# One TensorE loop of sixteen turns for two attention blocks: three units a turn, one accumulating output bank, and buffers of one slot per position

## The chip, the cores and the metric

The kernel runs on one core of one Trainium2 chip. The metric is the device time in microseconds (us). A kernel is executed several times beside the kernel before on the same chip. The profile is of one execution; its span is the time from the first to the last instruction, some 1.8 us less than the device time of the same execution.

## The reference, cut to what matters

Two independent attention blocks are computed for one new token each. Block A reads the whole cache of 8192 positions, block B only the last 2048.

```python
B, Sq, D = 4, 1, 512
Hq, Hkv, Sk, Dh = 32, 8, 8192, 128          # four query heads share one k/v head
q = (x @ wq).reshape(B, Sq, Hq, Dh).transpose(0, 2, 1, 3)
k = repeat(k_cache, 4, axis=1)              # block B: k_cache[:, :, Sk - W:, :], W = 2048
v = repeat(v_cache, 4, axis=1)
p = softmax(einsum("bhqd,bhkd->bhqk", q, k) * Dh ** -0.5)
o = einsum("bhqk,bhkd->bhqd", p, v)
out = o.transpose(...).reshape(B, Sq, Hq * Dh) @ wo
# result: concatenate([block A, block B], axis=-1)
```

In bfloat16 the caches of A are 134 MB, what B reads of its own is 34 MB, and the weights are 17 MB. There is little arithmetic per byte: each byte of K and V is used once.

## The kernel before: the parts that matter

Work is cut into units. A unit of A is one batch and one k/v head: 64 tiles of 128 positions, 2 MB of K and 2 MB of V. For each unit TensorE transposes K (`T`), makes scores (`S`), and later applies the probabilities to V (`PV`). The kernel before runs 8 large units of B first (2 MB of K each, too), then 32 units of A. K and V have four slots each.

```python
NKS, NVS, NKT, NPT = 4, 4, 4, 4
K_sb = sb("K_sb", [128, NKS, NT, DH], BF16)       # NT = 64 tiles
V_sb = sb("V_sb", [128, NVS, NT, DH], BF16)
KTB, STB, OTB, OPB = [0, 1, 2], [3, 4], [5, 6], 7 # PSUM banks: K transposed, scores, PV, output
...
TOKENS = [("T", 0), ("T", 1), ("OT",), ("T", 2), ("T", 3), ("S", 0), ("S", 1), ("X",),
          ("T", 4), ("T", 5), ("S", 2), ("S", 3), ("PV", 0), ("PV", 1), ("OL",),
          ("T", 6), ("T", 7), ("S", 4), ("S", 5), ("PV", 2), ("PV", 3), ("S", 6), ("S", 7), ("OPJ",)]
...
def sp_K(u):                                      # a slot is free when the unit four back is transposed
    waits = [("T", tjob_idx[(u - NKS, NB - 1)])] if u >= NKS else []
...
def sp_V(u):                                      # ... or when its PV is done
    waits = [("PV", (u - NVS) * NQ + NQ - 1)] if u >= NVS else []
```

The remaining tokens (`OT`, `OL`, `X`) stand for small jobs on the outputs and on the query projections. Most A units already run in a TensorE loop of four units a turn; the front and the end are unrolled. The output product `OPJ` of a group of four units is 4 matmuls of 512 columns for A, 16 for B.

## Time and profile before

| | before |
|---|---|
| device time, median (range) | 449.75 us (449.16 to 450.03, 4 runs) |
| span of the profiled run | 447.8 us |
| bytes read from memory | 184.56 MB |
| TensorE busy | 373.4 us, 83% of the span |
| mean granted TensorE clock | 0.797 |

The page cuts the span into 40 slices. Each digit is the busy share of a slice in tenths. PEclk is the granted TensorE clock in tenths, DMA the busy share of the 16 DMA engines, GB/s what they moved.

```profile
PE   0685199899676999988998998899889998988997
PEclk9996569989886899866596689867875986788596
DMA  8999999999999999999999999999999999999991
GB/s 337 411 415 438 413 421 415 420 421 423 423 422 421 425 422 425 424 429 427 427 427 430 430 424 426 430 428 427 429 426 427 426 430 429 426 424 430 430 403 65
```

The DMA row is what to look at: it is full from the second slice to the last but one. The TensorE row is nearly as full, yet it is not the limit. The groups of instructions (line, engine, operation, output<-input, shapes, count | busy us, mean ns | idle us just before them and what ended it) show transposes waiting for K:

```profile
L332 PE MATMUL ps<-identf,K_sb 128*128 128x128 f32 x1280 | 217.1, 329 | 32.9 <-DMA K_sb<-in_A_k_cache_dram 17.5
L483 PE MATMUL ps<-W,OL 128*4 128x512 bf16 x60 | 22.5, 537 | 4.8 <-DMA W<-in_B_wo_dram 4.8
```

The chain of work that ended last says the same by its shares of the span:

```profile
DMA 54%; PE 35%; issue 4%; ACT 3%; DVE 2%; POOL 0%; ACTq 0%; POOLq 0%
```

The DMA issues (SPq is the queue of SyncE, which issues the loads; count, KB each, median us from issue to landing) show how deep the queue is. A load waits about 30 us behind others, some 12 MB:

```profile
K_sb<-in_A_k_cache_dram SPq DMA_DIRECT2D x32, 2048.0 KB, 32.0
V_sb<-in_A_v_cache_dram SPq DMA_DIRECT2D x31, 2048.0 KB, 36.0
```

The busy times of the engines in stretches (us from the span's start; TensorE, its weight loads, DVE, ACT, POOL, then granted clock, DMA share, GB/s) give the rate of the stream and its end:

```profile
0.00:14.00 14.00, 0.00 (x0) 0.00 (x0) 0.18 (x4) 1.28 (x1) 2.03 (x12) 1.00 0.87 345
60.00:180.00 120.00, 102.38 (x1973) 88.60 (x1970) 61.43 (x136) 50.95 (x56) 10.34 (x30) 0.88 1.01 422
180.00:420.00 240.00, 217.52 (x3823) 202.49 (x3824) 105.46 (x243) 104.20 (x119) 22.14 (x71) 0.76 1.01 428
440.00:448.00 8.00, 5.17 (x126) 4.10 (x126) 2.08 (x7) 0.42 (x1) 0.46 (x2) 0.50 0.01 3
```

Data stop at 440 us. The last 7.8 us are TensorE's backlog and the output. The timeline (start, length, engine, line, ...; in brackets the idle time just before and what ended it, where `issue` stands for a time in which the engine waited for nothing that the profile shows) shows the backlog, 118 matmuls of the last two units:

```profile
440.17 3.31 PE L397 MATMUL ps<-PT,V_sb 128*128 128x4 bf16 x118 [0.82 <-issue]
443.79 1.86 PE L474 MATMUL ps<-W,OTg 128*4 128x256 bf16 x8 [0.31 <-DVE OTg L592]
```

The clock deserves a look too. A pair of transpose jobs (x8) takes 1.07 us when TensorE has been busy, and 1.97 us after it stood waiting for K:

```profile
285.80 1.07 PE L332 MATMUL ps<-identf,K_sb 128*128 128x128 f32 x8
289.84 1.97 PE L332 MATMUL ps<-identf,K_sb 128*128 128x128 f32 x8 [1.38 <-DMA K_sb<-in_A_k_cache_dram]
```

### The profile page before, as it was taken

The page shows a single profiled execution, that of the slowest core. Times are in us where ns is not written, and L with a number is a line of the kernel's source. Part 1 is how long each engine was busy: PE and PEld are TensorE (multiplying, and loading weights), DVE is VectorE, ACT ScalarE, POOL GpSimd, SP SyncE. Part 2 cuts the span into 40 slices and gives each one's busy share as a digit, 9 for nine tenths or more (in the row PEclk, how much of TensorE's full clock was granted, in tenths as well). Part 3 has the DMA queues.
Part 4 walks back from the last instruction along what each step waited for, and adds up shares of the span by engine and source line. Part 5 has one row for each costly group of instructions (what it writes and reads, how often), then busy time and mean ns, then how long its engine had stood idle before and what let it go on. Part 6 is the DMA issues. An engine that isn't in the chain of part 4 may idle for free.

```text
span 447.8 us, 14767 instructions
## 1 busy us (share of the span) xinstructions
PE 373.4 (83%) x6783; PEld 339.4 (76%) x6783; DVE 195.9 (44%) x451; ACT 179.2 (40%) x202; POOL 40.1 (9%) x126
## 2 busy tenths in 40 slices
PE   0685199899676999988998998899889998988997
PEld 0685199768561898878898887879878987878896
DVE  0354055656440455434363444344443544344363
ACT  1163045435330464434264434334442543435261
POOL 1100000001100011000010001000110100010010
PEclk9996569989886899866596689867875986788596
DMA  8999999999999999999999999999999999999991
GB/s 337 411 415 438 413 421 415 420 421 423 423 422 421 425 422 425 424 429 427 427 427 430 430 424 426 430 428 427 429 426 427 426 430 429 426 424 430 430 403 65
DMA packets 17270, 185.01 MB, mean 413 GB/s; under 512 B 1860, under 2 KB 2392, under 8 KB 4824
## 3 DMA queue, kind: packets, MB, share of 16 engines
q1 hardware_dynamic: 15096, 178.27, 94.4%
q10 hardware_dynamic: 2080, 6.30, 3.5%
q8 instruction: 22, 0.36, 0.3%
q14 instruction: 8, 0.07, 0.0%
q0 software_dynamic: 64, 0.01, 0.0%
HBM read 184.56 MB, written 0.01 MB: 412 GB/s over the span
## 4 chain that ended last, share of the span: by engine, by line
DMA 54%; PE 35%; issue 4%; ACT 3%; DVE 2%; POOL 0%; ACTq 0%; POOLq 0%
DMA K_sb<-in_A_k_cache_dram 41%; PE ps L332 19%; DMA W<-in_A_wq_dram 7%; DMA W<-in_B_wo_dram 6%; PE ps L397 6%; PE ps L371 5%; PE ps L483 3%; ACT KT_sb L341 3%; PE ps L278 1%; DVE KT_sb L340 1%; DVE Dt L543 0%; DVE M L505 0%; ACT PT L554 0%; PE ps L474 0%; PE ps L438 0%
## 5 line engine op out<-in xcount | busy, mean ns | idle before, releaser
L341 ACT ACTIVATE KT_sb<-ps 128x1024 bf16<-128x1024 bf16 x160 | 163.0, 1023 | 244.9 <-PE ps L332 243.1
L332 PE MATMUL ps<-identf,K_sb 128*128 128x128 f32 x1280 | 217.1, 329 | 32.9 <-DMA K_sb<-in_A_k_cache_dram 17.5
L332 PEld LDWEIGHTS ps<-identf,K_sb 128*128 128x128 f32 x1280 | 179.0, 170 | 46.2 <-DMA K_sb<-in_A_k_cache_dram 18.6
L340 DVE COPY KT_sb<-ps 128x512 int32<-128x512 int32 x160 | 110.4, 690 | 138.9 <-PE ps L332 137.7
L397 PE MATMUL ps<-PT,V_sb 128*128 128x4 bf16 (+1 forms) x2560 | 76.2, 165 | 3.6 <-DMA V_sb<-in_A_v_cache_dram 1.8
L371 PEld LDWEIGHTS ps<-RQc,KT_sb 128*128 128x128 bf16 x2048 | 72.9, 100 | 4.5 <-ACT KT_sb L341 1.2
L371 PE MATMUL ps<-RQc,KT_sb 128*128 128x8 bf16 x2048 | 74.3, 167 | 0.9 <-ACT KT_sb L341 0.8
L397 PEld LDWEIGHTS ps<-PT,V_sb 128*128 128x128 bf16 x2560 | 70.8, 97 | 3.9 <-DMA V_sb<-in_A_v_cache_dram 2.0
L575 POOL PARTITION_ALL_REDUCE LB<-L x40 | 17.3, 432 | 155.2 <-DVE L L566 155.2
L514 POOL PARTITION_ALL_REDUCE MB<-M x32 | 11.9, 371 | 173.3 <-DVE M L505 173.3
L483 PE MATMUL ps<-W,OL 128*4 128x512 bf16 x60 | 22.5, 537 | 4.8 <-DMA W<-in_B_wo_dram 4.8
L592 DVE TENSOR_TENSOR OTg<-ps,RL 128x4 bf16<-128x4 f32 (+1 forms) x40 | 6.9, 173 | 40.2 <-PE ps L397 40.2
L505 DVE TENSOR_REDUCE M<-ps 128x4 f32<-128x256 f32 (+1 forms) x40 | 19.1, 477 | 10.8 <-PE ps L371 10.8
L566 DVE TENSOR_REDUCE L<-PT 128x4 f32<-128x256 bf16 (+1 forms) x40 | 21.9, 547 | 3.3 <-ACT PT L554 2.8
L371 PE MATMUL ps<-RQB,KT_sb 128*128 128x16 bf16 x512 | 18.6, 171 | 2.1 <-issue 1.2
L371 PEld LDWEIGHTS ps<-RQB,KT_sb 128*128 128x128 bf16 x512 | 17.9, 99 | 3.0 <-issue 1.5
L554 ACT ACTIVATE PT<-Dt 128x256 bf16<-128x256 f32 (+1 forms) x40 | 18.1, 452 | 4.0 <-DVE Dt L543 2.0
L483 PEld LDWEIGHTS ps<-W,OL 128*4 128x4 bf16 x60 | 5.6, 104 | 15.3 <-issue 8.7
L278 PE MATMUL ps<-xT,W 128*128 128x4 bf16 x256 | 7.4, 165 | 10.9 <-DMA W<-in_A_wq_dram 10.6
L278 PEld LDWEIGHTS ps<-xT,W 128*128 128x128 bf16 x256 | 7.0, 101 | 11.1 <-DMA W<-in_A_wq_dram 10.7
L543 DVE TENSOR_TENSOR Dt<-ps,MB 128x256 f32<-128x256 f32 x32 | 13.3, 415 | 0.5 <-POOL MB L514 0.5
L257 PE MATMUL ps<-ident,xo_sb 4*128 4x4 bf16 x8 | 0.6, 170 | 14.2 <-POOL identf L617 14.2
(49 smaller groups left out, 64.6 us busy)
## 6 DMA issues: line engine op xcount, KB each, us to landing
K_sb<-in_A_k_cache_dram SPq DMA_DIRECT2D x32, 2048.0 KB, 32.0
V_sb<-in_A_v_cache_dram SPq DMA_DIRECT2D x31, 2048.0 KB, 36.0
K_sb<-in_B_k_cache_dram SPq DMA_DIRECT2D x16, 1024.0 KB, 28.2
V_sb<-in_B_v_cache_dram SPq DMA_DIRECT2D x16, 1024.0 KB, 28.2
W<-in_B_wq_dram SPq DMA_DIRECT2D x1, 4096.0 KB, 12.9
W<-in_A_wq_dram SPq DMA_DIRECT2D x1, 4096.0 KB, 30.0
W<-in_A_wo_dram ACTq DMA_DIRECT2D x8, 512.0 KB, 10.5
W<-in_B_wo_dram SPq DMA_DIRECT2D x1, 2048.0 KB, 29.1
```

The costliest lines, as they stand in the source:

```text
L278: ins = pe.matmul(out=bk[:, hl * Bn:(hl + 1) * Bn], lhsT=W1wq[:, c, hq * DH:(hq + 1) * DH], rhs=xT[:, P, c, :], start=(c == 0), stop=(c == ...
L332: ins = pe.transpose(out=bkf[:, pi * 128:(pi + 1) * 128], in_=K_sbf[:, slot, t0:t0 + 2, :].rearrange("p t d -> p (t d)"), identity=identf[ ...
L340: return e.tensor_copy(out=KT_sb.bitcast(I32)[:, tj % NKT, :], in_=bkf.bitcast(I32)[:, :])
L341: return e.activation(out=KT_sb[:, tj % NKT, :], in_=bk[:, :], func=ACTF.Copy)
L371: ins = pe.matmul(out=stb[:, t * CPT:(t + 2) * CPT], lhsT=ktv[:, pi, :, e], rhs=rhs, start=(e == 0), stop=(e == 1))
L397: ins = pe.matmul(out=otb[:, s * CPT:(s + 1) * CPT], lhsT=V_sb[:, vs, t, :], rhs=pt_cols(u, t * CPT, CPT), start=(j == 0), stop=(j == J - 1))
L483: ins = pe.matmul(out=opb[0:Bn, 0:D], lhsT=OL[:, i // REP, i % REP, :], rhs=wo_view[:, wg + i // REP, i % REP, :], start=(P == 1 and first ...
L505: return dve.tensor_reduce(out=M1[:, 0:NC].rearrange("p (s h) -> p s h", h=CPT), in_=stb[:, 0:NT * CPT].rearrange("p (s j h) -> p s h j", ...
L543: return dve.tensor_tensor(out=Dt[:, 0:NT * CPT].rearrange("p (s j h) -> p s j h", s=S, h=CPT), in0=stb[:, 0:NT * CPT].rearrange("p (s j h ...
L554: return act.activation(out=PT[:, u % NPT, 0:NW], in_=Dt[:, 0:NW], func=ACTF.Exp, scale=scale)
L566: return dve.tensor_reduce(out=L1[:, 0:NC].rearrange("p (s h) -> p s h", h=CPT), in_=PT[:, u % NPT, 0:NT * CPT].rearrange("p (s j h) -> p ...
L575: return pool.partition_all_reduce(LB[:, 0:NC], L1[:, 0:NC], channels=128, reduce_op=ReduceOp.add)
```

## The change

The intent is to make the whole TensorE program regular: 16 turns of the same loop, each with two units of A and one of B. A unit of B becomes two batches of one head (32 tiles, 1 MB of K). K and V get one slot per position of the turn: 160 tiles in place of 256. The scores get one bank in place of two, and K transposed gets four banks. Output weights are staged, copied by the Pool engine once a turn, and applied by 16 matmuls of 128 columns into one bank that accumulates over the whole kernel. Both query weights (8.4 MB) are loaded first. The diff, cut to its core (`...` marks cuts):

```diff
-    NKS, NVS, NKT, NPT = 4, 4, 4, 4
+    NPOS = 3
+    NTURN = 2 * HKV
+    NU = NPOS * NTURN
...
+    for t in range(NTURN):
+        g, bh = t // 2, t % 2
+        units.append(dict(P=0, g=g, b=2 * bh, CPT=REP, NT=NT))
+        units.append(dict(P=0, g=g, b=2 * bh + 1, CPT=REP, NT=NT))
+        units.append(dict(P=1, g=g, bh=bh, CPT=2 * REP, NT=NTB))
...
-        K_sb = sb("K_sb", [128, NKS, NT, DH], BF16)
-        V_sb = sb("V_sb", [128, NVS, NT, DH], BF16)
+        NTT = 2 * NT + NTB
+        K_sb = sb("K_sb", [128, NTT, DH], BF16)
+        V_sb = sb("V_sb", [128, NTT, DH], BF16)
...
-        KTB = [0, 1, 2]
-        STB = [3, 4]
-        OTB = [5, 6]
-        OPB = 7
+        KTB = [0, 1, 2, 3]
+        STB, OTB, EVB, OPB = 4, 5, 6, 7
...
+        def pe_OPJ(t):
+            ...
+                for P in range(2):
+                    for r in range(2):
+                        for j in range(4):
+                            ins = pe.matmul(out=banks_f[OPB][32 * j:32 * j + 8, 0:128], lhsT=OL[:, P, r, :],
+                                            rhs=Wfix[:, P, r, 128 * j:128 * j + 128], start=False, stop=False)
...
+        TOK_A = [("T", 0), ("T", 1), ("T", 2), ("T", 3), ("PV", 0), ("S", 0), ("S", 1), ("T", 4), ("T", 5), ("S", 2), ("S", 3),
+                 ("T", 6), ("T", 7), ("S", 4), ("S", 5), ("PV", 1), ("S", 6), ("S", 7)]
+        TOK_B = [("T", 0), ("T", 1), ("OT",), ("T", 2), ("T", 3), ("PV", 0), ("OL",), ("S", 0), ("S", 1), ("PV", 1), ("S", 2), ("S", 3), ("OPJ",)]
...                                            # in unit u the PV is that of unit u - 2
         def sp_K(u):
+            op("sp", dma(...), waits=[("T", tj_of[(u - NPOS, nt // 8 - 1)]) if u >= NPOS else None], inc=("K", u))
         def sp_V(u):
+            w = [pv_last(u - NPOS) if u >= 1 else None]
...
+        for P in range(2):
+            op("sp", dma(WQ_sb[P]..., WQ[P]...), inc=("wq", P))
+        for u in range(NU):
+            if u >= 2 and u < NU - 1:
+                sp_V(u - 2)
+            if u == NU - 2:
+                sp_K(u)
+                sp_K(u + 1)
+                continue
+            if u == NU - 1:
+                sp_V(u - 2)
+                sp_V(u)
+                sp_V(u - 1)
+                continue
+            sp_K(u)
+            if u % 6 == 3:
+                wo_load(u // 6)
```

The loads in the last lines go through one queue, in order, and a load that must wait for a free slot blocks all behind it. Units are numbered from 0 to 47 below; 45 and 46 are the A units of the last turn, 47 is its B unit, 44 the B unit before.

## The prediction

> **What bounds it now.** DMA. The page's slices show the 16 DMA engines at "9" from the second slice to the last but one, 403 to 438 GB/s, for 184.56 MB of input that cannot shrink. In the windows, 0 to 12 us average 345 GB/s, 180 to 420 us 423 to 432, and the stream ends near 440 us. The Trainium skill (DMA: Bandwidth & Descriptors, Specifications) gives a fabric ceiling of 435 GB/s; the trace sits 2% under it. The chain of waits agrees: 41% hops of K_sb from A_k_cache of about 30 us, transfers issued three units ahead. TensorE is 83% busy but not the limit: with a backlog a 64-tile unit takes 7.1 us; waiting for K it falls to half clock (8 transposes 1.97 us instead of 1.07) and takes about 9.6. DMA needs 9.9 us for an A unit (4.19 MB at 427 GB/s).
>
> **What the change does.** Bytes, tiles and shapes of T, S and PV stay. Removed: the unrolled TensorE front, the 60 output matmuls of 512 columns (537 ns, 22.5 us in all), one of two score banks, and buffer depth: K and V go from 256 tiles each to 160 (two A slots, one B). Added: 16 output matmuls of 128 columns and a Pool copy of weights a turn, both Wq (8.4 MB) loaded ahead of the first K, semaphore bookkeeping.
>
> TensorE per turn, estimated: 2 x 9.6 + 5 + 2 = 26 us at low clock, 20 at full. DMA per turn: 11 MB, 25.9 us. So DMA still binds, and TensorE speeds up when it lags.
>
> Does the shallow buffer starve DMA? When K of a first A unit lands, 6.3 MB (14.8 us) are still queued; the next issue comes when that unit's last PV is done, 9 to 10 us later, 2 more to data. It holds, with 3 us margin. Elsewhere 17.3 us are queued. The score bank now waits for the previous subtraction, but max, all-reduce, subtract and evictions (about 2.6 us) fit under 16 transposes and half a PV (2.7 us).
>
> **Off steady state.** Start: 15.7 MB go unblocked, to about 40 us. Unit 0 begins when both projections are done, about 29 us, and frees V1 and K3 at 37 to 39: a hole of 0 to 1.5 us. End: V of the last B unit waits for the previous B's PV, late in the next-to-last unit; 3.1 MB (7.4 us) are queued, a hole of about 2.5 us. Against that, the tail shrinks: before, 118 PV matmuls (3.3 us) ran after the last data and 8 us passed; after, I estimate 5 to 6.
>
> Sum: +0.5 +2.5 -2.5, a wash. Removed TensorE work buys nothing; it hides under DMA.
>
> **Prediction:** 449.5 us, range 445.5 to 456. Faster by over 2%: 0.03; within 2%: 0.90; slower by over 2%: 0.07.
>
> **What would show it.** DMA at 9 in nearly every slice, about 425 GB/s; K issue-to-landing falling from 32 us to about 15; one dip near 38 us and one near 430; TensorE idle before transposes put down to DMA of K; chain still DMA with shorter hops; output matmuls under 20 us.
>
> **What would make it wrong.** Slower: TensorE at half clock plus bookkeeping over 2 us a turn would eat the margin, the queue running dry once a turn (16 x 1 to 2 us, 465 to 480 us); or the Pool copy delays the sums' all-reduce and, through in-order DVE, the evictions. Faster: the early stretch (412 to 423 GB/s) reaching 430 when A and B mix, at most 5 us.

## The result, and the profile after

The time after is 452.35 us (451.73 to 453.84, 4 runs), against 449.75 us before. The ratio is 1.0065, with a 95% interval of 1.0045 to 1.0086. Ratios here are the mean time of one kernel's runs over that of the other's runs of the same rounds, so they are not quite the ratio of the medians quoted. The change is slower by about 3 us, which is well within 2%, and 452.35 lies in the predicted range.

Slices of the page, to be held against those of before:

```profile
PE   0369897896859699796959989697987968696895
PEclk9999789796879757895876959587787968798876
DMA  8999999999999999999999999999999999999945
GB/s 350 417 427 386 416 428 426 429 432 424 422 430 428 415 426 435 428 421 425 430 424 415 407 434 425 430 425 422 422 427 429 428 427 425 424 432 401 425 192 217
```

DMA is full again, except near the end, where two slices moved 192 and 217 GB/s. The fourth slice, 386, is a smaller dent. TensorE, meanwhile, shows digits of 6 and 7 where before it had 8 and 9. The groups say why: the transposes now wait 61.2 us, 59.2 of it for K of A, and the output product costs 7.0 us in place of 22.5 (2 x 0.6 us for the last head group come on top).

```profile
L326 PE MATMUL ps<-identf,K_sb 128*128 128x128 f32 x1280 | 212.4, 327 | 61.2 <-DMA K_sb<-in_A_k_cache_dram 59.2
L491 PE MATMUL ps<-Wfix,OL 128*8 128x128 bf16 x256 | 7.0, 234 | 0.0
```

The chain of waits, in its shares of the span:

```profile
DMA 61%; PE 35%; SPq 1%; DVE 1%; issue 1%; ACT 0%; POOL 0%
```

The DMA issues, in the columns of before:

```profile
K_sb<-in_A_k_cache_dram SPq DMA_DIRECT2D x32, 2048.0 KB, 17.1
V_sb<-in_A_v_cache_dram SPq DMA_DIRECT2D x31, 2048.0 KB, 15.5
```

The chain is more of DMA than before, and the queue is half as deep. The stretches, in the same columns as before:

```profile
0.00:14.00 14.00, 0.00 (x0) 0.00 (x0) 6.60 (x5) 1.28 (x1) 1.71 (x12) 1.00 0.91 368
38.00:44.00 6.00, 5.24 (x110) 5.13 (x107) 3.24 (x7) 3.27 (x5) 0.98 (x3) 1.00 0.95 355
60.00:180.00 120.00, 99.29 (x1953) 95.30 (x1951) 55.96 (x135) 51.81 (x61) 20.91 (x48) 0.80 1.01 427
180.00:420.00 240.00, 198.90 (x3892) 190.25 (x3889) 110.93 (x269) 100.77 (x120) 45.01 (x97) 0.79 1.01 424
430.00:436.00 6.00, 5.87 (x118) 5.67 (x117) 2.45 (x7) 3.10 (x4) 0.59 (x2) 0.77 0.11 46
445.00:450.00 5.00, 1.92 (x57) 1.32 (x48) 0.47 (x2) 0.00 (x0) 0.00 (x0) 0.50 0.03 8
```

From 60 to 420 us the stream runs at 425 GB/s, as before (422 and 428 there, 426 over the whole). So the shallow buffers cost nothing in the steady state. The difference lies at both ends. Estimated from these stretches, at 425 GB/s for a full stream:

| where | worked out from | us |
|---|---|---|
| first 14 us | 14 x (368 - 345) / 425 | -0.8 |
| dent near 40 us | 6 x (425 - 355) / 425 | +1.0 |
| dry stretch near 433 us | 6 x (425 - 46) / 425 | +5.4 |
| from last data to the end | (449.9 - 445.1) - (447.8 - 440.0) | -3.0 |
| sum, against the measured difference of spans, 449.9 - 447.8 = 2.1 | | +2.6 |

The DMA queue's own timeline shows the block at the end: an A unit's load of V was issued at 413.86 us, and then no load until 435.07 us, because the next one, V of unit 47, wants the slot of unit 44.

```profile
413.86 0.59 SPq L168 DMA_DIRECT2D V_sb<-in_A_v_cache_dram  x1
435.07 0.55 SPq L168 DMA_DIRECT2D V_sb<-in_B_v_cache_dram  x1
435.66 1.92 SPq L168 DMA_DIRECT2D V_sb<-in_A_v_cache_dram  x3
```

And TensorE's timeline shows why that slot came free late. Unit 46 waited for its K, started at half clock, and has the PV of unit 44 behind most of its own transposes:

```profile
426.70 3.67 PE L326 MATMUL ps<-identf,K_sb 128*128 128x128 f32 x16 [2.05 <-DMA K_sb<-in_A_k_cache_dram]
434.50 0.54 PE L368 MATMUL ps<-PT,V_sb 128*128 128x8 bf16 x16
```

The first line is sixteen transposes in 3.67 us, where 1.95 us is usual at full clock.

### The profile page after: what moved, and what is told of

Read it like the earlier page. It is cut to its first block, busy times and chain, and to the rows that moved or that the text cites. A ratio compares the mean times of both kernels' runs of the same rounds, so it can differ in the third digit from the quotient of the medians.

```text
span 449.9 us, 15730 instructions
## 1 busy us (share of the span) xinstructions
PE 356.6 (79%) x7136; PEld 340.7 (76%) x7136; DVE 204.9 (46%) x501; ACT 178.0 (40%) x210; POOL 74.4 (17%) x180
## 4 chain that ended last, share of the span: by engine, by line
DMA 61%; PE 35%; SPq 1%; DVE 1%; issue 1%; ACT 0%; POOL 0%
DMA K_sb<-in_A_k_cache_dram 54%; PE ps L326 23%; PE ps L368 6%; DMA WQB<-in_B_wq_dram 5%; PE ps L350 5%; DMA V_sb<-in_A_v_cache_dram 2%; SPq L168 1%; PE ps L255 1%; DVE RQB L286 0%; ACT KT_sb L335 0%; PE ps L501 0%; DVE M L384 0%; PE ps L270 0%; POOL MB L394 0%; PE ps L301 0%
## 5 line engine op out<-in xcount | busy, mean ns | idle before, releaser
L326 PE MATMUL ps<-identf,K_sb 128*128 128x128 f32 x1280 | 212.4, 327 | 61.2 <-DMA K_sb<-in_A_k_cache_dram 59.2
L368 PE MATMUL ps<-PT,V_sb 128*128 128x4 bf16 (+1 forms) x2656 | 82.3, 165 | 2.1 <-ACT PT L411 2.0
L368 PEld LDWEIGHTS ps<-PT,V_sb 128*128 128x128 bf16 x2656 | 80.0, 98 | 4.0 <-issue 2.4
L350 PEld LDWEIGHTS ps<-RQc,KT_sb 128*128 128x128 bf16 x2048 | 68.1, 98 | 7.4 <-ACT KT_sb L335 3.6
L511 POOL COPY Wfix<-Wst 128x2048 bf16<-128x2048 bf16 x14 | 27.4, 1956 | 0.0
L411 ACT ACTIVATE PT<-Dt 128x256 bf16<-128x256 f32 x48 | 19.6, 408 | 3.6 <-DVE Dt L404 3.6
L350 PE MATMUL ps<-RQcB,KT_sb 128*128 128x16 bf16 x512 | 17.7, 170 | 0.0
L437 DVE TENSOR_TENSOR OTg<-ps,RL 128x4 bf16<-128x4 f32 x28 | 4.7, 169 | 28.0 <-PE ps L368 28.0
L350 PEld LDWEIGHTS ps<-RQcB,KT_sb 128*128 128x128 bf16 x512 | 15.1, 97 | 0.3
L394 POOL PARTITION_ALL_REDUCE MB<-M1m x16 | 6.0, 376 | 34.4 <-DVE M1m L388 34.4
L452 POOL COPY RQc<-RQA 128x16 bf16<-128x16 bf16 x32 | 8.2, 258 | 15.7 <-DVE RQB L286 15.7
## 6 DMA issues: line engine op xcount, KB each, us to landing
K_sb<-in_A_k_cache_dram SPq DMA_DIRECT2D x32, 2048.0 KB, 17.1
```

Source lines behind the costliest of these rows:

```text
L326: ins = pe.transpose(out=banks_f[bk][:, pi * 128:(pi + 1) * 128], in_=K_sbf[:, t0:t0 + 2, :].rearrange("p t d -> p (t d)"), identity=ident ...
L350: ins = pe.matmul(out=banks_f[STB][:, t * CPT:(t + 2) * CPT], lhsT=ktv[:, pi, :, e], rhs=rq[:, e, :], start=(e == 0), stop=(e == 1))
L368: ins = pe.matmul(out=banks_f[bank][:, 0:CPT], lhsT=V_sb[:, T0P[pos] + t, :], rhs=PT[:, u % NPT, t * CPT:(t + 1) * CPT], start=(t == 0), s ...
L394: op("pool", lambda pool: pool.partition_all_reduce(MB[:, 0:CPT], src[:, 0:CPT], channels=128, reduce_op=ReduceOp.max), waits=[w], inc=("a ...
L411: op("act", lambda act: act.activation(out=PT[:, u % NPT, :], in_=Dt[:, :], func=ACTF.Exp, scale=scale), waits=[("sub", u), pv_last(u - NP ...
L511: op("pool", lambda pool: pool.tensor_copy(out=Wfix[:, :, :, :], in_=Wst[:, g % 2, :, 2 * hh:2 * hh + 2, :]), waits=[("wst", g), ("OPJ", t ...
```

## The experiments

My theory after reading the traces: TensorE work hides under DMA throughout, the shallow queue holds in the steady state, and the loss of 3 us is made at the two places where an in-order load waits for a late slot. Rivals: (1) the shallow buffers cost bandwidth all along; (2) the loop, its bookkeeping and the Pool copy cost time that ate a real gain from the smaller output product; (3) the six dry microseconds are themselves the loss. All outputs are right.

### The changed kernel again (e0_after)

The changed kernel, with no edit, beside the first repairs on one chip.

> The changed kernel itself, unaltered, so that the others have it from the same chip and rounds. Both theories: 452 to 453 us, about 0.65% over before. DMA dry from about 430.5 to 436.5 us of the span, a smaller dip near 40 us.

Measured: 452.29 us (6 runs, 450.33 to 453.04), ratio to before 1.0044 (1.0023 to 1.0064). It reproduces. The profiled run shows something that the first profile did not: a start dent of 2.8 us in place of 1.0 (38 to 44 us at 223 GB/s). In this run TensorE did unit 0 at half clock (a pair of transpose jobs 1.95 us, in place of 1.07), so the V load that waits for it was issued at 40.55 us and not at 38.47:

```profile
35.16 1.95 PE L326 MATMUL ps<-identf,K_sb 128*128 128x128 f32 x8
40.55 0.34 SPq L168 DMA_DIRECT2D V_sb<-in_A_v_cache_dram  x1
```

### K ahead of V at the end (e1_kfirst)

```diff
-            if u >= 2 and u < NU - 1:
+            if u >= 2 and u < NU - 2:
                 sp_V(u - 2)
             if u == NU - 2:
                 sp_K(u)
+                sp_V(u - 2)
                 sp_K(u + 1)
```

> One swap in the DMA queue: K of the next-to-last unit is issued ahead of V of the B unit before it (1 MB). Theory (the loss is at the end: TensorE sits idle 2 us for that K, starts at half clock, so its PV of the last-but-one B unit and with it the release of the last V loads come late): the idle time before that unit falls from 2 us to near 0, the unit runs at full clock, the dry stretch of DMA shrinks from 6 us to about 2, and the whole falls by 3 to 4.5 us, to about 448.5. Rival (the shallow buffers cost bandwidth all along, or loop bookkeeping does): no change, 452.

Measured: 450.99 us (6 runs, 448.53 to 454.18), ratio 1.0038 (1.0011 to 1.0065). By time this is inconclusive: the runs spread over 5.65 us, and the median fell by 1.3 us where 3 to 4.5 were expected. The profiled run, the fastest of the six with a span of 446.7 us, shows each step as expected. Unit 46 begins without a wait and at full clock, and the blocked load is issued at 431.19 us in place of 435.07:

```profile
425.06 1.94 PE L326 MATMUL ps<-identf,K_sb 128*128 128x128 f32 x16
431.19 0.54 SPq L168 DMA_DIRECT2D V_sb<-in_B_v_cache_dram  x1
```

That the slower runs of this kernel differ in the clock or in the start dent is plausible but was not seen, as they were not profiled. The swap gets a cleaner test below.

### The last V loads into a dead buffer (e2_vdead)

The buffer of the first query weights is unused after the start. Units 46 and 47 put their V there, and the loads wait for no PV. (V of unit 47 gets a semaphore of its own, as two loads on one semaphore would be in flight.)

```diff
+        Vend = WQ_sb[0][:, :].rearrange("p (t d) -> p t d", d=DH)
...
-                    ins = pe.matmul(out=banks_f[bank][:, 0:CPT], lhsT=V_sb[:, T0P[pos] + t, :],
+                    vt = Vend[:, t + (0 if u == UA else NT), :] if u >= UA else V_sb[:, T0P[pos] + t, :]
+                    ins = pe.matmul(out=banks_f[bank][:, 0:CPT], lhsT=vt,
...
-            w = [pv_last(u - NPOS) if u >= 1 else None]
+            w = [pv_last(u - NPOS) if 1 <= u < UA else None]
...                                            # and the two DMA destinations likewise
```

> The last two V loads go into the dead query-weight buffer, so they wait for no PV and the DMA queue does not run dry at the end. If the 6 us hole itself is what costs: about -5 us, 447. My theory, read from the chain after: TensorE reaches the last PV only at about 445 us anyway, because the next-to-last unit begins late, so the hole is off the critical path: -0.3 to -1 us, 451.5 to 452, with the last V landed near 440 us and TensorE busy to the end.

Measured: 450.28 us (6 runs, 448.66 to 452.01), ratio 1.0013 (0.9991 to 1.0036), 1.7 us under e0_after by the means (450.36 and 452.03), though the intervals overlap. That is more than the 0.3 to 1 us of my theory and far less than the 5 us of rival 3. The dry stretch is gone: 430 to 436 us moved 410 GB/s, and the stream ended at about 439 us in place of 445. So six microseconds of dry DMA were taken away and less than two of them came back in time; rival 3 falls. What decides in its place is TensorE's own chain: the PV of unit 47 begins at 441.12 us, 2 us after the last data, and what it waited for last is the exponential on ACT (2.02 us), as in the changed kernel. The stretch, and the PV:

```profile
430.00:436.00 6.00, 5.87 (x111) 5.51 (x108) 3.73 (x10) 3.73 (x5) 0.97 (x3) 1.00 0.98 410
441.12 1.84 PE L372 MATMUL ps<-PT,WQA 128*128 128x8 bf16 x64 [2.02 <-ACT PT L415]
```

### The first output weights early (e3_wo_early)

```diff
             sp_K(u)
-            if u % 6 == 3:
+            if u == 2:
+                wo_load(0)
+            if u % 6 == 3 and u > 3:
                 wo_load(u // 6)
```

> The first output weights (1 MB, they wait for nothing) are issued before the V load that blocks the queue at the start, not after it. Theory (hole of 1.1 us near 40 us, and everything after it is DMA-bound): the dip near 40 us goes, the whole falls by about 1 us, to 451.3. Rival (the dip is not on the path, the end alone decides): no change.

Measured: 450.14 us (6 runs, 448.84 to 450.58), ratio 1.0004 (0.9987 to 1.0021): 2.1 us under e0_after by the means (449.90 and 452.03), and the intervals do not overlap. 38 to 44 us moved 384 GB/s in place of the 223 of e0_after, which is worth 6 x (384 - 223) / 425 = 2.3 us; the blocked V load was again issued as late as 40.42 us, but this time a megabyte was queued that needed nothing. These are the stretches of e0_after and of this run:

```profile
38.00:44.00 6.00, 5.89 (x123) 5.75 (x122) 3.16 (x6) 3.29 (x5) 0.61 (x2) 1.00 0.70 223
38.00:44.00 6.00, 5.89 (x123) 5.75 (x122) 3.16 (x6) 3.28 (x5) 0.75 (x3) 1.00 0.99 384
```

The gain is twice what I expected. In both of these profiles unit 0 ran at half clock. At full clock the dent is smaller (1.0 us in the first profile). How often unit 0 ran at which clock is known of the profiled runs alone, so why the mean fell by as much as 2.1 us stays open.

### TensorE work put back (e4_work)

```diff
                         for j in range(4):
+                            if P == 0 and r == 0 and j == 0:
+                                for _ in range(8):
+                                    pe.matmul(out=banks_f[EVB][0:32, 128:512], lhsT=ident[:, 0:32],
+                                              rhs=RQA[...].rearrange(...)[:, 0:384], start=True, stop=True)
```

> Eight idle matmuls of 384 columns are added to every turn's output product, about 1.3 us a turn at full clock and 2.6 at half, 21 to 42 us of TensorE time in all: what the change took off TensorE is put back. The result stays right. Theory (TensorE work hides under DMA): no loss in the turns; only the last turn's 1.3 us show at the end, so 452 to 454 us. Rival (the removed work was worth its time, and something else in the change ate the gain): 465 us or more.

Measured: 452.81 us (4 runs, 452.56 to 453.12), ratio 1.0083 (1.0063 to 1.0102). The added matmuls were busy for 33.9 us, more than the output product had ever cost, and the time stands within 0.4% of the changed kernel (1.0044 and 1.0065 in its two sets of rounds). Rival 2 is refuted as to its gain: the TensorE work that the change removed was worth next to nothing, and the 33.9 us cost 0.8 to 1.8, by which of the two sets it is compared with.

```profile
L493 PE MATMUL ps<-RQA,ident 128*32 128x384 bf16 x128 | 33.9, 427 | 0.0
403.00:404.00 1.00, 1.00 (x31) 1.00 (x28) 0.49 (x2) 0.09 (x1) 0.00 (x0) 1.00 0.24 98
```

The expectation of no loss in the turns did not hold throughout. In the profiled run DMA nearly ran dry from 403 to 406 us (the second line is its first microsecond): 400 to 420 us moved 376 GB/s, against 410 in e0_after, which is worth 20 x (410 - 376) / 425 = 1.6 us. In the last turn nothing was lost: the last PV of B began at 443.93 us, in e0_after at 443.88.

### A delay once a turn, with the shallow and with the deep queue (e5_delay_after, e6_delay_before, e10_delay_before_b)

```diff
+        def pe_extra():
+            def fn(pe):
+                for _ in range(16):
+                    ins = pe.matmul(out=banks_f[EVB][0:32, 128:512], lhsT=ident[:, 0:32],
+                                    rhs=RQA[...].rearrange(...)[:, 0:384], start=True, stop=True)
+                return ins
+            op("pe", fn)
+
         def pe_PV(u, half, after):
+            if half == 1 and (u + 2) % NPOS == 0:
+                pe_extra()
```

In the kernel before the same function runs in `pe_PV(u, c)`, `if c == 2 and NU_B < u < L - 1 and u % 4 == 1` (e6), or `... < L - 2 ...` (e10).

> Sixteen idle matmuls of 384 columns, 2.6 us at full clock and 5.1 at half, before the last PV of the first A unit of every turn, in the changed kernel: a delay of the V and K issue at the one point where the queue has least left. Theory (shallow queue, margin there about 1 us by the trace): DMA runs dry once a turn for 1 to 3 us, 16 turns, so 465 to 500 us. Rival (only total TensorE time counts, 20 plus 2.6 of 25.9 us a turn): 452 to 455.

> The same sixteen matmuls in every fourth A unit of the kernel before, 10 or 8 times, ahead of its third PV part. Theory (four slots, some 12 MB queued ahead): no change, 449 to 450.5 us. If it slows by over 3 us, buffer depth is not what tells the two kernels apart under delay.

Measured after: 458.04 us (4 runs, 456.26 to 459.15), ratio 1.0185 (1.0157 to 1.0213). Measured before: 452.81 us (4 runs, 451.58 to 453.58), ratio 1.0076 (1.0053 to 1.01). Both expectations failed. After, the delay costs 1.4 points of ratio over e0_after, about 6 us, which is far less than the 13 to 48 us I gave it and more than the rival's 3. Before, it was not free. The trace of e6 shows at once where: DMA from 60 to 420 us was untouched (422 and 427 GB/s), but the last of the eight doses stands between the last data and the end.

```profile
439.04 2.77 PE L385 MATMUL ps<-RQA,ident 128*32 128x384 bf16 x16
441.74 0.96 PE L407 MATMUL ps<-PT,V_sb 128*128 128x4 bf16 x32
```

So the kernel before was run again without that dose.

> The delay in the kernel before again, without the last dose, which the trace of the first try shows at 439.1 us on the closing chain after the last data. Theory (deep queue: delays inside the stream cost nothing, only that last dose did): within 0.2% of before. Rival (delays cost in the deep queue too): 2 us or more over.

Measured: 449.92 us (4 runs, 448.79 to 450.76), ratio 1.0005 (0.9978 to 1.0032). Seven doses of 2.7 us inside the deep stream cost nothing that can be measured. In the shallow stream of e5, the stretches from 60 to 420 us fell to 419 GB/s, against 426 and 424 in e0_after:

```profile
60.00:180.00 120.00, 109.77 (x2020) 99.71 (x2019) 56.02 (x134) 51.60 (x62) 20.33 (x46) 0.88 1.00 419
180.00:420.00 240.00, 216.04 (x3978) 197.14 (x3974) 108.96 (x265) 99.80 (x118) 43.36 (x97) 0.85 1.00 419
```

That is 120 x 7 / 426 + 240 x 5 / 424 = 4.8 us over 14 doses, 0.3 us a turn: the queue ran visibly dry in three of them (near 94, 253 and 410 us) and thinned in others. The shallow queue has a margin of about the size of this delay, 2.7 us. The deep one has more: at 0.3 us each its seven doses would have cost 2.4 us, and the interval of e10 ends at 1.4. Rival 1 is right about what shallow buffers risk, and wrong about what they cost here.

### The three repairs together (e7_combo, e11_combo_again)

The edits of e1, e2 and e3 in one kernel, as their diffs above; e11 is the same file again.

> The three repairs together: K first, last V loads into the dead buffer, first output weights early. Theory: DMA dry nowhere until the end, last V landed near 439 us, the whole 446.5 to 448 us, under the kernel before (449.75). If the repairs overlap fully: 448.5.

Measured: 447.42 us (6 runs, 446.88 to 448.75), ratio 0.9959 (0.9943 to 0.9975). The kernel beats both: 0.4% under the kernel before and 0.8 to 1.1% under the changed kernel. DMA ran dry nowhere between 14 and 437 us, and the last data came near 438 us. It was run a second time as the partner of the next two.

> The three repairs together, byte for byte the kernel of the combo run, as the partner on this chip for the two variants of it: ratio to before 0.996.

Measured: 448.07 us (6 runs, 447.32 to 449.2), ratio 0.9977 (0.9957 to 0.9997). The size wavers between 0.2 and 0.4%, the sign does not.

### Filling TensorE's wait (e8_fill)

```diff
+        def pe_fill():                          # twelve matmuls as in e5
...
                     pe_OPJ(t)
+                    pe_fill()
```

> The combo plus twelve idle matmuls of 384 columns (1.9 us at full clock) after the output product of every turn, where TensorE otherwise waits about 4 us for K and falls to half clock. Theory (with DMA dry nowhere, the end is TensorE's own chain, from K of the unit before the next-to-last on, and that unit runs at half clock: 10.4 us instead of 7.5): if the filler keeps the clock up, 1.5 to 2.5 us faster than the combo, ratio to before about 0.991; the last turn's filler fits into the 2 us wait for the last exponential. Rival (the end of the DMA stream decides): no change or slower by up to 2 us. If the mean clock does not rise, undecided.

Measured: 448.42 us (6 runs, 446.86 to 451.1), ratio 0.9985 (0.9956 to 1.0013), against 0.9977 of the combo: no gain. The mean clock rose as wanted, from 0.810 to 0.896, and unit 45, which in the combo began at half clock (sixteen transposes in 3.67 us), now began at full clock. But TensorE then stood waiting for the next load:

```profile
416.42 1.97 PE L327 MATMUL ps<-identf,K_sb 128*128 128x128 f32 x16 [1.19 <-DMA K_sb<-in_A_k_cache_dram]
424.31 1.97 PE L327 MATMUL ps<-identf,K_sb 128*128 128x128 f32 x16 [0.85 <-DMA K_sb<-in_A_k_cache_dram]
437.37 3.12 PE L503 MATMUL ps<-RQA,ident 128*32 128x384 bf16 x12
```

Unit 46 began at 424.31 us, and in the combo at 424.40. The last turn's filler, which I thought free, ran until the last PV began (440.42 us, against 438.79 in the combo). My theory of this run falls: before unit 46 the extra speed had nothing to work on, because the load had not landed. The last filler stood in the closing chain as well, so this run is no clean test of the end.

### The combo without the swap (e9_no_kfirst)

The combo with the edit of e1 taken back:

```diff
-            if u >= 2 and u < NU - 2:
+            if u >= 2 and u < NU - 1:
                 sp_V(u - 2)
             if u == NU - 2:
                 sp_K(u)
-                sp_V(u - 2)
                 sp_K(u + 1)
```

> The combo without the swap of K and V. Theory: in the combo TensorE reaches the next-to-last unit some 2 to 5 us after its K could land, so the swap is idle there: same as the combo within 0.5 us. If the swap has its own worth: 2 us slower than the combo.

Measured: 449.85 us (6 runs, 448.51 to 451.2), ratio 1.0007 (0.9983 to 1.003), 1.6 us over the combo by the means of the same rounds (449.76 and 448.13). The expectation was that the swap is idle there; it is not. In the trace unit 46 waits for K again and starts at half clock:

```profile
426.61 3.63 PE L327 MATMUL ps<-identf,K_sb 128*128 128x128 f32 x16 [1.68 <-DMA K_sb<-in_A_k_cache_dram]
```

So of the three repairs each has its worth at its place: the start about 2 us (e3), the swap 1 to 2 us (this pair; the intervals of its two kernels just overlap), and the dead buffer 1.7 us alone by the means, with an interval that overlaps too. They don't simply add up: the start and the dead buffer without the swap (e9, 449.76 us by the mean) are no faster than the start alone (e3, 449.90, in other rounds), and only with the swap does the time fall under the kernel before.

## Why the prediction was right, point by point, and where it was not

**DMA binds, before and after: right.** The stream is full in the slices of both kernels, and the rate over 60 to 420 us is equal within 1% (426 and 425 GB/s). The Trainium skill (DMA: Bandwidth & Descriptors, Bandwidth) gives 425 GB/s for a load of 16 MB issued from GpSimd; these two kernels, with loads of 1 and 2 MB from SyncE, show 422 to 428.

**Removed TensorE work buys nothing: right, and shown.** Waiting for K of A rose from 17.5 us to 59.2 us, and e4 put 33.9 us of work back at a cost of 0.8 to 1.8 us.

**The shallow buffers hold: right; the margin of 3 us was about right too.** Issue to landing of K was predicted at 15 us and measured at 17.1. After the traces I thought the margin was nearer 1 us, and e5 spoke for the first figure: 2.7 us of delay a turn took only 0.3 us a turn. Counted in the first trace (bytes issued less bytes moved, at 425 GB/s), loads worth 1.4 to 6.3 us (median 3.7) were still queued at the late V issue of these turns. Some 1.5 us pass from issue to data, so the margin was about 2 us in the middle and almost none once.

**Score bank, Pool copy and loop bookkeeping: harmless, as predicted.** The Pool copy takes 1.96 us and stands in TensorE's wait for K; no wait of the chain is put down to it. No run took it away by itself, so this rests on the traces.

**Start dent of 0 to 1.5 us near 38 us: right in place, too narrow in size.** It was 1.0 us in one profile and 2.8 us in another, as the clock in unit 0 was full or half. I had reckoned with one clock.

**Dry stretch near 430 us: the step that was mis-sized.** The prediction said "3.1 MB (7.4 us) are queued, a hole of about 2.5 us". The hole was about 6 us long and 5.4 us worth. The far end of it was right: the prediction's two numbers put the next data 9.9 us after the landing of K of unit 46 (426.70 us), and they came 9.8 us after it, at 436.5 (the unit began at half clock, and its PV ended 8.3 us after the landing). What failed is the near end: the queue lasted not 7.4 us after the landing but 3.7 (DMA thinned from 430.4 us). The packed trace shows why, as it keeps the time of each of a load's 16 semaphore increments. For K of unit 46, fourteen of them came from 422.99 to 424.33 us, and the last two at 426.38 and 426.66. For V of unit 45, the last load in the queue, fourteen came from 430.36 to 431.69, and the last two at 433.71 and 433.99. In order, each increment follows its counterpart by 7.3 to 7.4 us, just what the prediction gave for 3.1 MB. But the landing is told by the last increment, and by then the first fourteen parts of the load had been done for 2.3 to 3.7 us. The skill (DMA: Bandwidth & Descriptors, Why a DMA increments its semaphore by 16 and not by 1) says that the 16 engines finish a transfer independently and the semaphore is full only with the last of them, so a landing can be told while other engines are already on later loads; the trace agrees, with these figures. Why two parts lag is not known.

**Shorter tail: right in direction, a little under in size.** From the last data to the end it was 7.8 us before and 4.8 us after; the prediction had 8 and 5 to 6.

**The sum: +0.5 +2.5 -2.5 was predicted, a wash.** Measured it is -0.8 +1.0 +5.4 -3.0. The verdict (within 2%) and the range held. The centre was 2.9 us low, which is also the excess of the hole (5.4 for 2.5). That the two match is luck: the other three terms were together off by -0.8, and the centre lay 0.75 below the prediction's own sum (449.75 + 0.5), which makes up for it. And the experiment on that hole teaches more than its size: taking it away whole gave back 1.7 us (e2), because TensorE's chain from K of the last units ends at nearly the same time. Two chains ran side by side at the end, and a repair had to shorten both, which the swap of two loads does for the K side and the dead buffer for the V side.

**"Faster: the early stretch reaching 430 when A and B mix":** the early stretch rose from 422 to 427 GB/s, but the late one fell from 428 to 424. The rate evened out and nothing was added; that the mixing of A and B did it was not tested.

## What to carry to other kernels

When the DMA stream is full from end to end, count what a change does to the queue, not to the engines: here 33.9 us of TensorE work could be added at a cost of about 2, while reordering a few loads, and giving the last two another buffer, gave 0.7 to 1.1%. Halving the depth of the queue cost nothing here in the steady state, where each slot was given back before the queue ran out, but it left the start and the end, and more so a start at half clock, without reserve: look for the in-order load that waits for a late slot, and put before it something that waits for nothing. Do not count a queue from the landing that a semaphore tells: here most of the queue was then 2 to 4 us shorter. Ask of each hole which chain ends last beside it, because closing a hole of 6 us gave here only the 1.7 us that the second chain allowed.

## What the Trainium skill lacked or had wrong

- TensorE: Matmul & The Clock Gate (Part 1, and Why this matters for your kernels) has the clock fall after an idle window of about 3.4 us and advises against gaps over about 3 us. Here shorter gaps were followed by half clock: 2.05 us before unit 46 (sixteen transposes in 3.67 us, 1.95 at full clock) and 1.38 us in the kernel before (eight in 1.97 us, 1.07 just ahead of the gap). Gaps of 0.85 and 1.19 us in e8 were not.
- The same page (Part 3) says that matmuls on different column strips of the array run side by side, and gives measured gains for 512 columns. It has none for 128: here 16 output matmuls of 128 columns on four strips took 0.40 us at full clock, 25 ns each, where the page (Part 1) gives 55.6 ns for one after the other.
- DMA: Bandwidth & Descriptors has no figure for how far apart the 16 increments of one load come when the queue is full. Here those of K of unit 46 came 3.7 us apart, first to last, with fourteen within 1.3 us; so the 3.1 MB queued behind it lasted only 3.7 us after it was told, half of what the bytes take at 425 GB/s.
